# Moving the starts of TensorE's moving operands inside their SBUF tiles in a fused attention and mixture-of-experts kernel

## The chip, the cores and the metric

One NeuronCore of one Trainium2 chip runs the whole kernel. The metric is the device time of one execution in microseconds. A run of the kernel before is shown by its median over three runs; a separate execution, taken with the hardware profiler, gives the trace.

## The reference

Two branches read the same x (2048 tokens, 512 features) and are mixed by a gate:

```
x = A_x;  g = sigmoid((x * gate_w).sum(-1))
a = attention(x):   qkv = x @ wqkv (512 x 1536), 32 heads of 16,
                    each position looks at 8 keys: itself and every second one before (window 8, dilation 2)
                    softmax, weighted sum of v, then @ wo
b = experts(x):     logits = x @ w_gate; the best 2 of 8 experts per token
                    out += gate * (silu(x @ w1[e]) @ w2[e])      w1: 512 x 1376, w2: 1376 x 512
return g * a + (1 - g) * b
```

## The kernel before, in words

All products keep float32 accuracy with operands split in two (a high and a low part in fp32r): a product is hi*hi + hi*lo + lo*hi, so three matmuls stand where one would.

*Stage 1, qkv.* The columns of wqkv come in four chunks c of 384. For each chunk 16 token blocks j pass through `qkv_mm`: 12 matmuls each (4 k slices, 3 combinations), the x block stationary (`xh`, `xl`), the weights `WH[c]`, `WL[c]` moving. Chunk 0 carries ten more columns (the expert logits and the gate), so its k slices lie 394 columns apart and its matmuls have 394 columns. The tiles of the weights have two places each for high and low, used in turn, in the pool `pa`.

*Routing and attention.* VectorE does routing, then attention by element-wise products, as filler: `att_fill` puts its pieces between other VectorE work by a cost model of TensorE's time (T_MM and others), so the order on VectorE is fixed when the program is built.

*Stage 2, experts.* Experts are ranked by load; rank R has room for CAPS[R] tokens: 558, 548, 534, 500, 500, 496, 484, 484. They run in the order ORD = 3, 0, 1, 2, 5, 6, 7, 4. An expert has 11 units f (128 of the 1376 hidden columns each). For a unit, `g1_mm` issues the first product (line 859): w1 stationary, the gathered rows of x (`xgh`, `xgl`, 4 k slices) moving, 12 matmuls of CAPS[R] columns, or 24 of half the width when that is over 512. `g1_act` (lines 869 to 873) makes h = silu in the tile `hs`, high part from column 0, low part from column 640; two hs tiles of 1152 columns serve in turn. `g2_mm` issues the second product. For R in TURN (0, 1, 2, 5, 6, 7) w2 is stationary and hs moves, MAIN[R] columns (496, 484, 472 for R = 0, 1, 2), lines 898, 899, 901; the first unit's first matmul of each of the four groups has 512. The tokens past MAIN[R] are done by two matmuls of 512 columns in which hs is stationary (lines 903, 904). For R = 3 and 4 hs is stationary and w2 moves, always 512 columns (lines 889 to 892). The rows lie in tiles of 4 x 576 columns; where CAPS[R] is at most 512 the k slices are 512 columns apart, from the tile's first column. In each unit the order on TensorE is: first product of the next unit, then second product of this one.

*Stage 3, output.* `wo_mm` multiplies the attention output with wo for 16 blocks j; the results of blocks 0 to 2 lie in the three PSUM banks "h", the rest in the five banks "y". `mix(j)` on VectorE joins block j with the sum over experts (read back from DRAM in five loads, `load_acc`) and sends it out. MIX says after which block's matmuls which blocks are mixed.

Tiles of one pool and tag share a place in SBUF, one after the other. In the pool `at`, "acc", "o" and "qt" hold attention tiles from the second chunk on; before that "acc" holds `ii` (an iota from which `ident` and `before` are made) and "o" the gate weights `wgs`.

Of the kernel before, what the change touches and what calls it, by code (L numbers as in the profile page):

```python
# [7 lines left out]
F32 = mybir.dt.float32  # L8
F32R = mybir.dt.float32r
# [9 lines left out]
P = 128  # L19
S = 2048  # L20
D = 512
NJ = S // P
KD = D // P
# [5 lines left out]
NF = 11  # L29

CAPS = [558, 548, 534, 500, 500, 496, 484, 484]
MAIN = [496, 484, 472] + CAPS[3:]

ORD = [3, 0, 1, 2, 5, 6, 7, 4]
# [2 lines left out]
NB = 5  # L37
N5 = sum(c > 4 * P for c in CAPS)
W_ = 4 * len(CAPS) + N5
NOV = 40  # L40
# [1 line left out]
FC = [min(P, F - P * f) for f in range(NF)]  # L42
CRPAD, PAPAD = 176, 32
NWARM, NWARM2 = 26, 4
MIX = {5: (0,), 6: (1, 2, 3), 7: (4,), 8: (5, 6), 9: (7, 8)} | {j: (j - 1,) for j in range(10, NJ - 1)} | {NJ - 1: (NJ - 2, NJ - 1)}
SPLIT = {1: (8, 10, 12, 14), 2: (4, 6, 8, 10)}
IDLE = 2.0
FILL = 0.5
# [16 lines left out]
def kernel(  # L65
# [37 lines left out]
    def py(name):  # L103
        return ps.tile([P, 512], F32, tag="y", bufs=5, name=name)

    def ph(name):
        return ps.tile([P, 512], F32, tag="h", bufs=3, name=name)
# [3 lines left out]
    at = phT.enter_context(tc.tile_pool(name="at", bufs=1, side="right"))  # L111
# [5 lines left out]
    pa = phA.enter_context(tc.tile_pool(name="pa", bufs=1, side="left"))  # L117
# [4 lines left out]
    for i in range(2):  # L122
        t = pa2.tile([P, 2, D], F32, tag="xr", bufs=2, name=f"xr{i}")
        XR[2 * i], XR[2 * i + 1] = t[:, 0], t[:, 1]

    NW = [394, 384, 384, 384]
# [9 lines left out]
                              wq[:, k, :, c * P:(c + 1) * P])  # L136


    wgs = at.tile([P, KD * 9], F32, name="wgs", tag="o")
    nc.scalar.dma_start(wgs[:, :KD * 8], w_gate.rearrange("(p k) e -> p (k e)", p=P))  # L140
    nc.scalar.dma_start(wgs[:, KD * 8:], gate_w.rearrange("(p k) -> p k", p=P))
    for j in range(2):
# [44 lines left out]
    for r in range(E):  # L187
        nc.gpsimd.memset(caps[:, r:r + 1], float(CAPS[r]))
    src = cp.tile([P, 2, NJ, 2], I32, name="src")
# [31 lines left out]
    def clear_acc(j):  # L221
        n = 4 if j == 12 else 2
        if j % 2 == 0 and j < 14:
            nc.sync.dma_start(acc_d[:S].rearrange("(p j) d -> p j d", p=P)[:, j:j + n], zer[:, None, :].to_broadcast([P, n, D]))

    def split_w(c, k, vec=False):
        if c not in WH:
            for W, n in ((WH, "wh"), (WL, "wl")):
                t = pa.tile([P, 1600], F32R, tag=n, bufs=2, name=f"{n}{c}")
                W[c] = t[:, :KD * NW[c]].rearrange("p (k c) -> p k c", k=KD)  # L230
        if k is None:
            return
        if vec:
            nc.vector.tensor_copy(WH[c][:, k, :384], WR[c][:, k, :384])
        else:
            nc.scalar.activation(WH[c][:, k, :384], WR[c][:, k, :384], AF.Copy)
        nc.vector.tensor_tensor(WL[c][:, k, :384], WR[c][:, k, :384], WH[c][:, k, :384].bitcast(F32), op=OP.subtract)
# [147 lines left out]
    def slots():  # L385
# [42 lines left out]
        V.tensor_scalar(io, cap, 4.0 * P, 4.0 * P, op0=OP.is_le, op1=OP.mult)  # L428
        for c, m in zip(CAPS[:N5], MAIN):
            V.tensor_scalar(rr, cap, float(c), float(m), op0=OP.is_equal, op1=OP.mult)  # L430
# [326 lines left out]
    def blocks(R):  # L757
        return [P] * 3 + [MAIN[R] - 3 * P] + [CAPS[R] - MAIN[R]] * (CAPS[R] > MAIN[R])

# [12 lines left out]
    HS, XGH, XGL = [], {}, {}  # L772
# [5 lines left out]
    def turn_rows(R, b):  # L778
        if b == 0:
            pool = B["01"[ORD.index(R) % 2]]  # L780
            w = 576 if CAPS[R] > 4 * P else 4 * P
            for X, tag in ((XGH, "xgh"), (XGL, "xgl")):
                X[R] = pool.tile([P, KD * 576], F32R, tag=tag, name=f"{tag}{R}")[:, :KD * w].rearrange("p (k c) -> p k c", k=KD)
        m = blocks(R)[b]
        n = -(-m // 32)
        o = min(b * P, MAIN[R])
        s = slice(o, o + m)
        raw = B["0"].tile([P, KD, P], F32, tag="xraw", bufs=2, name=f"xraw{R}_{b}")[:, :, :32 * n]
        V.transpose(raw.rearrange("p k (t i) -> p t k i", i=32), XG[R, b][:, :n].rearrange("p t (k q) -> p t k q", k=KD))
        clk["dve"] += T_S  # L790
        return XGH[R][:, :, s], XGL[R][:, :, s], raw[:, :, :m]
# [71 lines left out]
    def g1_act(R, f, i):  # L863
        tiles, halves = PH.pop((R, f))
        C = CAPS[R]
        hs = HS[i % 2]
        s = B["1"].tile([P, 576], F32, tag="hsf", bufs=2, name=f"hsf{R}_{f}")
        for t, (o, n) in zip(tiles, halves):
            nc.scalar.activation(hs[:, o:o + n], t[:, :n], AF.Silu)  # L869
        for t, (o, n) in zip(tiles, halves):  # L870
            nc.scalar.activation(s[:, o:o + n], t[:, :n], AF.Silu)  # L871
        n = MAIN[R]
        V.tensor_tensor(hs[:, 640:640 + n], s[:, :n], hs[:, :n].bitcast(F32), op=OP.subtract)  # L873
        if C > n:
            V.tensor_tensor(hs[:, n + 64:C + 64], s[:, n:C], hs[:, n:C].bitcast(F32), op=OP.subtract)
# [3 lines left out]
    def g2_mm(R, f, i):  # L879
        if f == 0:  # L880
            PY[R] = [py(f"py{R}_{b}") for b in range(4 + (CAPS[R] > MAIN[R]))]
        hs = HS[i % 2]
        wh, wl = WS.pop((2, R, f))
        y = PY[R]
        st, sp = f == 0, f == NF - 1
        if R not in TURN:

            for b in range(4):
                nc.tensor.matmul(y[b], hs[:, b * P:b * P + P], wh, start=st, stop=False)
                nc.tensor.matmul(y[b], hs[:, b * P:b * P + P], wl, start=False, stop=False)  # L890
            for b in range(4):
                nc.tensor.matmul(y[b], hs[:, 640 + b * P:640 + b * P + P], wh, start=False, stop=sp)
            return
        n = MAIN[R]
        for m in range(4):
            a, b = wh[:, m * P:m * P + P], wl[:, m * P:m * P + P]
            k = 4 * P if st else n
            nc.tensor.matmul(y[m][:, :k], a, hs[:, :k], start=st, stop=False)  # L898
            nc.tensor.matmul(y[m][:, :n], b, hs[:, :n], start=False, stop=False)  # L899
        for m in range(4):  # L900
            nc.tensor.matmul(y[m][:, :n], wh[:, m * P:m * P + P], hs[:, 640:640 + n], start=False, stop=sp)  # L901
        if CAPS[R] > n:
            nc.tensor.matmul(y[4], hs[:, n:n + P], wh, start=st, stop=False)
            nc.tensor.matmul(y[4], hs[:, n:n + P], wl, start=False, stop=sp)
# [95 lines left out]
    for c in range(1, 4):  # L1000
        for j in range(NJ):
# [41 lines left out]
            if c == 3:  # L1043
                los()
                for g, u in NEXTW.pop(j - 1, ()):
                    g(*u)
                if j == 10:
                    prep_w1(*units[0])
                    NEXTW[j] = ((next_w1, units[0]),)
                if 7 <= j < 7 + len(blocks(ORD[0])):  # L1050
                    split_rows(*turn_rows(ORD[0], j - 7))
                if j == 13:

                    nc.scalar.activation(act0, ones[:, :1], AF.Silu)
                if 10 < j < 15:
                    u = units[(j - 10) // 2]
                    a, b = (prep_w1, next_w1) if j % 2 == 0 else (prep_w2, next_w2)
                    a(*u)
                    NEXTW[j] = ((b, u),)
# [5 lines left out]
    HS += [pb.tile([P, 1152], F32R, name=f"hs{i}") for i in range(2)]  # L1065
    n = 512 - CAPS[ORD[0]]
    for t in HS:
        for o, m in ((512, P), (1152, n)):
            V.tensor_tensor(t[:, o - n:o - n + m], ident[:, :m], ident[:, :m], op=OP.subtract)
    los()  # L1070
    WO = {}
# [30 lines left out]
    load_w2(ORD[0], 3)  # L1102
    NU = len(units)
    g1_act(*units[0], 0)
    for i, (R, f) in enumerate(units):
        C = CAPS[R]
# [6 lines left out]
        if R in NEXT:  # L1113
            N1 = NEXT[R]

            n = len(blocks(N1))
# [24 lines left out]
        if new_x:  # L1141
            rows = turn_rows(NEXT[R], f - 3)
# [7 lines left out]
        if i + 1 < NU:  # L1150
            g1_mm(*units[i + 1])
            g1_act(*units[i + 1], i + 1)
        if f == 3:
            read_back(f)
        if new_x:
            split_rows(*rows)
        g2_mm(R, f, i)
        out = y_out(R) if f == NF - 1 else iter(())
        next(out, None)
# [33 lines left out]
    def mix(j):  # L1193
        r = AG[j]
        n = D if j < NJ - 1 else D // 2
        for c in range(0, D, n):
            V.scalar_tensor_tensor(r[:, c:c + n], PA[j][c][:, :n], GG[:, j:j + 1], r[:, c:c + n],
                                   op0=OP.mult, op1=OP.add)
            nc.sync.dma_start(ot[:, j, c:c + n], r[:, c:c + n])
# [10 lines left out]
    for j in range(NJ):  # L1210
# [6 lines left out]

        for jj in MIX.get(j, ()):
            mix(jj)
# [7 lines left out]
    with tc.For_i(0, nov, 1) as it:  # L1227
# [25 lines left out]
        p = ph("pvx")  # L1253
# [5 lines left out]
        for f in range(NF):  # L1259
            m = FC[f]  # L1260
# [5 lines left out]
        for f in range(NF):  # L1266
            m = FC[f]
# [33 lines left out]
```

## Time and profile before

| | |
|---|---|
| median of three runs | 700.82 us (699.17 to 701.88) |
| the profiled execution's own time | 701.67 us |
| its span, first to last instruction | 699.9 us |
| TensorE matmuls (PE) busy | 685.4 us, 98% |
| VectorE (DVE) busy | 628.5 us, 90% |
| ScalarE (ACT) busy | 339.1 us, 48% |
| GpSimd (POOL) busy | 310.1 us, 44% |
| mean granted TensorE clock | 0.992 of 2.4 GHz |

Busy time is the union of an engine's instructions. The records of neighbouring matmuls overlap, so how long one matmul holds TensorE is read from the distance of their starts and not from the mean of one record.

### The profile page before, as it was taken

The page shows a single profiled execution, that of the slowest core. Times are in us where ns is not written, and L with a number is a line of the kernel's source. Part 1 is how long each engine was busy: PE and PEld are TensorE (multiplying, and loading weights), DVE is VectorE, ACT ScalarE, POOL GpSimd, SP SyncE. Part 2 cuts the span into 40 slices and gives each one's busy share as a digit, 9 for nine tenths or more (in the row PEclk, how much of TensorE's full clock was granted, in tenths as well). Part 3 has the DMA queues.
Part 4 walks back from the last instruction along what each step waited for, and adds up shares of the span by engine and source line. Part 5 has one row for each costly group of instructions (what it writes and reads, how often), then busy time and mean ns, then how long its engine had stood idle before and what let it go on. Part 6 is the DMA issues. An engine that isn't in the chain of part 4 may idle for free. (4 is left out here: it accounts for less than half of the span.)

```text
span 699.9 us, 11125 instructions
## 1 busy us (share of the span) xinstructions
PE 685.4 (98%) x3624; PEld 615.1 (88%) x3624; DVE 628.5 (90%) x782; ACT 339.1 (48%) x789; POOL 310.1 (44%) x351
## 2 busy tenths in 40 slices
PE   9999959989999999999999999999999999999997
PEld 9999959988889999999999998888888888888886
DVE  6859609999999999999999999998999999999793
ACT  5643204345644445455545454646644654465450
POOL 5400275056158506746663475475368230050400
PEclk9999979999999999999999999999999999999999
DMA  7868937638675837767867687978769884871493
GB/s 186 234 173 275 290 84 196 159 112 225 154 182 163 171 78 174 197 180 129 218 170 190 134 199 204 181 205 219 187 139 239 219 159 123 236 127 58 60 347 136
DMA packets 103565, 124.45 MB, mean 178 GB/s; under 512 B 10145, under 2 KB 73985, under 8 KB 103121
## 3 DMA queue, kind: packets, MB, share of 16 engines
q1 hardware_dynamic: 93072, 104.22, 55.2%
q0 software_dynamic: 10144, 19.48, 15.4%
q8 instruction: 29, 0.48, 0.3%
q14 instruction: 32, 0.25, 0.1%
q10 hardware_dynamic: 288, 0.02, 0.0%
HBM read 87.12 MB, written 36.57 MB: 177 GB/s over the span
## 5 line engine op out<-in xcount | busy, mean ns | idle before, releaser
L766 POOL DMA_INDIRECT xg<-in_A_x_dram,TQ x133 | 183.6, 1381 | 112.5 <-DVE rt_tk L519 51.1
L869 ACT ACTIVATE hs<-phh 128x500 fp32r<-128x500 f32 (+5 forms) x121 | 54.9, 481 | 156.8 <-PE phh L859 144.8
L898 PE MATMUL py<-hs,w2h 128*128 128x484 f32 (+3 forms) x264 | 100.7, 382 | 0.0
L899 PE MATMUL py<-hs,w2l 128*128 128x484 f32 (+2 forms) x264 | 100.6, 381 | 0.0
L859 PE MATMUL phh<-xgl,w1h 128*128 128x500 f32 (+5 forms) x484 | 96.3, 332 | 1.6 <-DVE xgl L804 1.6
L859 PE MATMUL phh<-xgh,w1h 128*128 128x500 f32 (+5 forms) x484 | 96.3, 332 | 0.5 <-ACT xgh L794 0.5
L859 PE MATMUL phh<-xgh,w1l 128*128 128x500 f32 (+5 forms) x484 | 96.2, 331 | 0.0
L911 POOL DMA_INDIRECT acc_d<-yr,TI x24 | 50.1, 2086 | 93.8 <-ACT yr L935 89.2
L859 PEld LDWEIGHTS phh<-xgh,w1h 128*128 128x128 f32 x484 | 78.6, 188 | 10.8 <-ACT xgh L794 0.8
L317 PE MATMUL pq<-wh,xh 128*128 128x384 f32 (+1 forms) x248 | 84.7, 342 | 1.9 <-issue 1.9
L317 PE MATMUL pq<-wl,xh 128*128 128x384 f32 (+1 forms) x248 | 83.9, 340 | 2.3 <-issue 2.3
L837 ACT ACTIVATE w2h<-w2r 128x512 fp32r<-128x512 f32 (+1 forms) x88 | 55.5, 631 | 60.6 <-PE py L901 20.5
L859 PEld LDWEIGHTS phh<-xgl,w1h 128*128 128x128 f32 x484 | 76.7, 188 | 9.2 <-DVE xgl L804 2.0
L859 PEld LDWEIGHTS phh<-xgh,w1l 128*128 128x128 f32 x484 | 76.8, 188 | 7.3
L317 PE MATMUL pq<-wh,xl 128*128 128x384 f32 (+1 forms) x248 | 77.6, 340 | 3.2 <-issue 3.2
L327 ACT ACTIVATE stg<-pq 128x128 f32<-128x128 f32 x192 | 40.1, 282 | 69.4 <-PE pq L317 47.7
L628 DVE TENSOR_TENSOR pr<-qt,kt 128x2048 f32<-128x2048 f32 x32 | 73.1, 2293 | 0.1
L631 DVE TENSOR_REDUCE lg<-pr 128x128 f32<-128x2048 f32 x32 | 72.4, 2271 | 0.0
L901 PE MATMUL py<-hs,w2h 128*128 128x484 f32 (+2 forms) x264 | 68.5, 381 | 0.0
L873 DVE TENSOR_TENSOR hs<-hsf,hs 128x484 fp32r<-128x484 f32 (+3 forms) x88 | 58.9, 670 | 5.2 <-ACT hsf L871 5.1
L804 DVE TENSOR_TENSOR w2l<-w2r,w2h 128x512 fp32r<-128x512 f32 (+1 forms) x88 | 60.5, 687 | 0.0
L804 DVE TENSOR_TENSOR w1l<-w1r,w1h 128x512 fp32r<-128x512 f32 (+1 forms) x88 | 59.3, 674 | 0.1
(235 smaller groups left out, 1282.3 us busy)
## 6 DMA issues: line engine op xcount, KB each, us to landing
w2r<-in_B_w_dram SPq DMA_DIRECT2D x40, 512.0 KB
w1r<-in_B_w_dram SPq DMA_DIRECT2D x96, 192.0 KB
qkv<-stg SPq DMA_DIRECT2D x24, 512.0 KB
ysc<-yt SPq DMA_DIRECT2D x24, 256.0 KB
yr<-ysc SPq DMA_DIRECT2D x6, 1024.0 KB
kt<-qkv SPq DMA_DIRECT2D x32, 156.0 KB
vt<-qkv SPq DMA_DIRECT2D x32, 156.0 KB
qt<-qkv SPq DMA_DIRECT2D x32, 128.0 KB
```

The costliest lines, as they stand in the source:

```text
L317: nc.tensor.matmul(p[:, :n], xx[j][:, s], ww[c][:, k, :n], start=(q == 0), stop=(q == 3 * KD - 1))
L628: V.tensor_tensor(pr, qb, custom(k, 4 * u * DH, [[2 * DH, 2], [1, 1024]]), op=OP.mult)
L631: V.tensor_reduce(lg[:, :, 2 * u - 2:2 * u].rearrange("p a w -> p w a"), prs[u - 1].rearrange("p w (a d) -> p w a d", d=16), axis=AX.X, op ...
L766: nc.gpsimd.indirect_dma_start(out=t[:, T], out_offset=None, in_=xq, in_offset=bass.IndirectOffsetOnAxis(ap=TQ[:, T, col:col + 1], axis=0))
L804: V.tensor_tensor(l, t, h.bitcast(F32), op=OP.subtract)
L837: nc.scalar.activation(hh, tt, AF.Copy)
L859: nc.tensor.matmul(t[:, :n], w[:, k], xx[:, k, o:o + n], start=(k == 0 and i == 0), stop=(k == KD - 1 and i == 2))
L869: nc.scalar.activation(hs[:, o:o + n], t[:, :n], AF.Silu)
L873: V.tensor_tensor(hs[:, 640:640 + n], s[:, :n], hs[:, :n].bitcast(F32), op=OP.subtract)
L898: nc.tensor.matmul(y[m][:, :k], a, hs[:, :k], start=st, stop=False)
L899: nc.tensor.matmul(y[m][:, :n], b, hs[:, :n], start=False, stop=False)
L901: nc.tensor.matmul(y[m][:, :n], wh[:, m * P:m * P + P], hs[:, 640:640 + n], start=False, stop=sp)
```

## The change

Four things move; no product, no column count and no order of the experts changes.

1. Where the moving operands of the experts begin. `SHIFT`: the rows of expert 3 begin 48 columns into their tiles, those of 4 at 32, of 6 and 7 at 48. `HSHIFT`: h of experts 0, 1, 2, 6 and 7 begins 8 columns into the hs tile (the low part at 648). One more strip of each hs tile, 12 columns, is zeroed at the start (columns 628 to 640).
2. The weights of chunk 0 get tiles of their own, in the places "acc" and "o" of `at`, from column 112, with the k slices 448 columns apart instead of 394. Chunks 1 and 3 share one place in `pa`, chunk 2 has the other.
3. `wgs` is put into the place "qt" instead of "o".
4. `MIX`: block 3 is mixed first and block 4 next, then 0 and 1, then 2; before it was 0, then 1, 2 and 3, then 4.

```
+SHIFT = {3: 48, 4: 32, 6: 48, 7: 48}
+HSHIFT = {0: 8, 1: 8, 2: 8, 6: 8, 7: 8}
...
-MIX = {5: (0,), 6: (1, 2, 3), 7: (4,), 8: (5, 6), 9: (7, 8)} | {j: (j - 1,) for j in range(10, NJ - 1)} | {NJ - 1: (NJ - 2, NJ - 1)}
+MIX = {5: (3,), 6: (4, 0, 1), 7: (2,), 8: (5, 6), 9: (7, 8)} | {j: (j - 1,) for j in range(10, NJ - 1)} | {NJ - 1: (NJ - 2, NJ - 1)}
...
-    wgs = at.tile([P, KD * 9], F32, name="wgs", tag="o")
+    wgs = at.tile([P, KD * 9], F32, name="wgs", tag="qt")
...
+    def w_tile(n, c):
+        t = pa.tile([P, 1600], F32R, tag=f"{n}{c % 2}", name=f"{n}{c}")
+        return t[:, :KD * 384].rearrange("p (k c) -> p k c", k=KD)
+
     def split_w(c, k, vec=False):
         if c not in WH:
             for W, n in ((WH, "wh"), (WL, "wl")):
-                t = pa.tile([P, 1600], F32R, tag=n, bufs=2, name=f"{n}{c}")
-                W[c] = t[:, :KD * NW[c]].rearrange("p (k c) -> p k c", k=KD)
+                if c == 0:
+                    for i in (2, 1):
+                        W[i] = w_tile(n, i)
+                    t = at.tile([P, 2048], F32R, tag={"wh": "acc", "wl": "o"}[n], name=f"{n}0")
+                    W[c] = t[:, 112:112 + KD * 448].rearrange("p (k c) -> p k c", k=KD)
+                elif c == 3:
+                    W[c] = w_tile(n, c)
...
-                X[R] = pool.tile([P, KD * 576], F32R, tag=tag, name=f"{tag}{R}")[:, :KD * w].rearrange("p (k c) -> p k c", k=KD)
+                X[R] = pool.tile([P, KD * 576], F32R, tag=tag, name=f"{tag}{R}")[:, SHIFT.get(R, 0):][:, :KD * w].rearrange("p (k c) -> p k c", k=KD)
...
-        hs = HS[i % 2]
+        hs = HS[i % 2][:, HSHIFT.get(R, 0):]
...
-        for o, m in ((512, P), (1152, n)):
+        for o, m in ((512, P), (640, n), (1152, n)):
```

The line of hs changes alike in `g1_act` and `g2_mm`.

## Rows read from the trace of the kernel before

**Rows 1.** The page's first part, busy us of each engine (share of the span) and instructions.

```profile
PE 685.4 (98%) x3624; PEld 615.1 (88%) x3624; DVE 628.5 (90%) x782; ACT 339.1 (48%) x789; POOL 310.1 (44%) x351
```

**Rows 2.** Busy time by stretch. Columns: stretch, its length, busy us (instructions) of PE, PEld, DVE, ACT and POOL, granted clock, busy share of the DMA engines, GB/s. The second stretch holds the eight experts.

```profile
93.00:108.00 15.00, 7.58 (x26) 6.35 (x25) 2.69 (x2) 3.78 (x17) 12.09 (x23) 0.66 0.20 55
156.50:660.00 503.50, 503.50 (x2618) 442.55 (x2619) 491.04 (x559) 266.33 (x531) 252.29 (x219) 1.00 0.72 170
```

**Rows 3.** Starts of matmuls on TensorE, from the timeline at ten places. Columns: start in us, length of the merged records in us, engine, line, operation, out<-in, stationary and moving shape, how many are merged. Between two rows of a pair lie only matmuls of the first row's shape: 12 for chunk 0 (394 columns), 12 for chunk 2 (384), 12 and 2 for expert 0, 24 for expert 1, 12 for expert 2, 24 for expert 5, 24 for expert 6, 12 and 12 for expert 4.

```profile
14.92 0.34 PE L317 MATMUL pq<-wh,xh 128*128 128x394 f32 x1
...
17.10 0.34 PE L317 MATMUL pq<-wh,xh 128*128 128x394 f32 x1
...
85.92 0.33 PE L317 MATMUL pq<-wh,xh 128*128 128x384 f32 x1
...
88.00 0.33 PE L317 MATMUL pq<-wh,xh 128*128 128x384 f32 x1
...
235.84 0.39 PE L898 MATMUL py<-hs,w2h 128*128 128x496 f32 x1
...
238.53 0.40 PE L903 MATMUL py<-w2h,hs 128*128 128x512 f32 x1
...
239.00 0.94 PE L859 MATMUL phh<-xgh,w1h 128*128 128x280 f32 x6
...
301.08 1.17 PE L859 MATMUL phh<-xgh,w1h 128*128 128x274 f32 x8
...
304.12 0.38 PE L898 MATMUL py<-hs,w2h 128*128 128x484 f32 x1
...
370.99 0.37 PE L898 MATMUL py<-hs,w2h 128*128 128x472 f32 x1
...
373.55 0.39 PE L903 MATMUL py<-w2h,hs 128*128 128x512 f32 x1
...
432.06 1.04 PE L859 MATMUL phh<-xgh,w1h 128*128 128x496 f32 x4
...
437.34 0.60 PE L859 MATMUL phh<-xgh,w1h 128*128 128x496 f32 x2
...
484.91 1.04 PE L859 MATMUL phh<-xgh,w1h 128*128 128x484 f32 x4
...
490.16 0.38 PE L859 MATMUL phh<-xgh,w1h 128*128 128x484 f32 x1
...
600.69 1.06 PE L859 MATMUL phh<-xgh,w1h 128*128 128x500 f32 x4
...
603.37 0.39 PE L889 MATMUL py<-w2h,hs 128*128 128x512 f32 x1
...
606.09 0.38 PE L859 MATMUL phh<-xgh,w1h 128*128 128x500 f32 x1
```

**Rows 4.** Groups of instructions by line and form. Columns: line, engine, operation, out<-in, shapes, count | busy us, mean ns of one | idle us before them.

```profile
L899 PE MATMUL py<-hs,w2l 128*128 128x484 f32 x132 | 50.3, 381 | 0.0
...
L859 PE MATMUL phh<-xgh,w1h 128*128 128x500 f32 x88 | 23.4, 387 | 0.5 <-ACT xgh L794 0.5
...
L1069 DVE TENSOR_TENSOR hs<-ident 128x12 fp32r<-128x12 f32 x2 | 0.3, 157 | 0.0
```

**Rows 5.** The start of the kernel on VectorE (the second reader of ii) and on ScalarE (the first write of the first chunk's weight tile). In brackets: idle us before it, and what ended the wait.

```profile
1.28 0.72 DVE L179 TENSOR_SCALAR before<-ii 128x128 bf16<-128x128 int32 x1
...
3.82 0.23 ACT L244 ACTIVATE wh<-wgs 128x32 fp32r<-128x32 f32 x1 [0.64 <-DMA wgs<-in_B_w_gate_dram]
```

**Rows 6.** VectorE at the first expert: the strips of hs are zeroed, then the first low part of h is made.

```profile
160.91 0.64 DVE L1069 TENSOR_TENSOR hs<-ident 128x128 fp32r<-128x128 f32 x4
162.18 0.68 DVE L873 TENSOR_TENSOR hs<-hsf,hs 128x500 fp32r<-128x500 f32 x1 [0.62 <-ACT hsf L871]
```

**Rows 7.** The output stage: the mixes of blocks 1, 2 and 3 on VectorE, then TensorE as block 8 begins (line 1189 at 673.84).

```profile
671.66 2.04 DVE L1197 SCALAR_TENSOR_TENSOR ag<-pa,GG,ag 128x512 f32<-128x512 f32 x3
...
673.54 0.39 PE L1191 MATMUL pa<-woh,w1l_o 128*128 128x512 f32 x1
673.84 0.47 PE L1189 MATMUL pa<-woh,w1h_o 128*128 128x512 f32 x1
674.15 0.40 PE L1190 MATMUL pa<-wol,w1h_o 128*128 128x512 f32 x1
```

**Rows 8.** VectorE's waits from 110 to 660 us (who waited <- for whom: us in total, times, longest), and the timeline of expert 7: VectorE's low part of h (line 873), and the matmuls that read it (line 901).

```profile
DVE hs L873 <- ACT hsf L871: 5.1, 7, 1.3
DVE mx L652 <- ACT lg L642: 4.1, 4, 1.6
...
553.77 0.69 DVE L652 TENSOR_REDUCE mx<-lg 128x64 f32<-128x512 f32 x1 [0.82 <-ACT lg L642]
...
562.01 0.66 DVE L873 TENSOR_TENSOR hs<-hsf,hs 128x484 fp32r<-128x484 f32 x1
...
562.81 1.07 PE L901 MATMUL py<-hs,w2h 128*128 128x484 f32 x4
...
567.18 0.66 DVE L873 TENSOR_TENSOR hs<-hsf,hs 128x484 fp32r<-128x484 f32 x1
...
568.09 1.04 PE L901 MATMUL py<-hs,w2h 128*128 128x484 f32 x4
```

**Rows 9.** TensorE between 93 and 104.5 us, one of its matmuls and the wait before it.

```profile
98.54 0.48 PE L317 MATMUL pq<-wh,xl 128*128 128x384 f32 x1 [2.31 <-issue]
```

More of the change, by code (lines that the diff above doesn't have):

```diff
@@ L881, in g2_mm @@
             PY[R] = [py(f"py{R}_{b}") for b in range(4 + (CAPS[R] > MAIN[R]))]
-        hs = HS[i % 2]
+        hs = HS[i % 2][:, HSHIFT.get(R, 0):]
         wh, wl = WS.pop((2, R, f))
```

## The prediction

> **What bounds the kernel now.** I read the page first. TensorE's matmuls are busy for 685.4 of 699.9 us and VectorE for 628.5 [rows 1]; the reader is to see that TensorE hardly pauses, so that other engines matter only where it waits for them, and that VectorE comes next. The table by stretches says where: from 156.5 to 660 us, the eight experts, PE is busy in 503.50 of 503.50 us and VectorE in 491.04 [rows 2]. No wait is left there to be removed. So the end is set by how many matmuls there are and how far apart they start. The program issues the same 3624 matmuls after the change; only the distance of their starts can move.
>
> That distance is not the 381 or 387 ns that the grouped rows give as the mean of one (those overlap); it is read from the timeline, as time between two starts divided by the matmuls between them [rows 3]. The granted clock is 1.00 there [rows 2], which is 2.4 GHz, so n columns need n/2.4 ns; what is above that I call the surplus:
> - 512 columns, last expert: 606.09 - 603.37 = 2.72 us for 12, 226.7 ns, surplus 13.3. 496, expert 5: 437.34 - 432.06 = 5.28 us for 24, 220.0, surplus 13.3. 384: 88.00 - 85.92 for 12, 173.3, surplus 13.3.
> - 484, expert 6: 490.16 - 484.91 for 24, 218.75, surplus 17.1. 500, expert 4: 603.37 - 600.69 for 12, 223.3, surplus 15.0. 472, expert 2: 373.55 - 370.99 for 12, 213.3, surplus 16.7. 496, but expert 0: 238.53 - 235.84 for 12, 224.2, surplus 17.5. 394: 17.10 - 14.92 for 12, 181.7, surplus 17.5.
> - the halves of a 548-slot expert: 304.12 - 301.08 for 24, 126.7, surplus 12.5. And the two 512-column matmuls behind expert 0, whose weights lie in the hs tile: 239.00 - 238.53 for 2, 235, surplus 21.7.
>
> So 484 columns cost nearly as much as 496, and 496 cost 220.0 in one expert and 224.2 in another: the column count alone does not give the surplus. The second group of widths is just the one the change moves.
>
> At this point a rule of the Trainium skill speaks against the change. "TensorE: Matmul & The Clock Gate", section "Back-to-back issue gap", gives the distance from the columns alone (N/2.4 + 2.5 ns), and Part 2, "What happens when you issue a matmul", has the weight load on a port of its own that takes nothing from the moving stream. By it a tile's place could not matter and the matmuls would gain nothing. The rows do not agree: it would put 496 columns at 209.2 ns in both experts, where they stand at 220.0 and 224.2.
>
> **The change, part by part.** The matmuls moved, from the loops (11 units of an expert, 12 matmuls of a product; the groups by form agree: 132 for one of three second-product parts, 88 for one of three parts of the first product [rows 4]): with 484 columns 2 x 11 x 12 = 264 in the first product and, in the second, 3 x 132 less the 12 that read 512, 384; with 500, 264; with 496 in expert 0 and with 472 in expert 2, 132 less 4 each, 128; with 394, 16 blocks x 12 = 192.
> - *The unknown price* is the surplus at the new places, which no row shows. Bounds: below, the next lower multiple of 6.67 ns, because every steady distance in [rows 3] whose tiles all start alike is one (173.3, 220.0, 226.7 are 26, 33 and 34 of them; 223.3 is the mean of 33 and 34): 484 at 213.3, 500 at 220.0, 472 at 206.7, 394 at 173.3. Above, the worst surplus seen, 21.7. In between lies the surplus that the cleanest full-width groups have, 13.3, and I take it, since the moved matmuls have the same operands as those groups and are nearest to them in width.
> - 484: 218.75 to 215.0, 648 x 3.75 ns = 2.43 us. 500: 223.3 to 221.7, 264 x 1.7 = 0.44. Expert 0's 496: 224.2 to 220.0, 128 x 4.2 = 0.53. 472: 213.3 to 210.0, 128 x 3.3 = 0.43. The 22 matmuls behind expert 0: 235 to 226.7, 0.18.
> - 394: the wider tile (stride 448 for 394) lets all four k slices start alike, as the 384 ones do; I take the whole step above 13.3, 27 x 6.67 = 180.0, so 192 x 1.7 = 0.32 us.
> - *Where that tile now lies.* It takes the places of "acc" and "o". It must wait for the readers of ii, the last of which ends at 1.28 + 0.72 = 2.00 us; its first write comes at 3.82, held by the load of the gate weights [rows 5]. Cost nothing; without that cover this write would be later by what the wait exceeds 3.82. The loads and issues of wgs are the same two. In the second stretch cols0 and cols1 take the places after the first chunk's last matmul, long before.
> - *The zeroed strip.* Two more VectorE instructions of 128x12 at 157 ns, 0.31 us [rows 4], in front of the first hs. VectorE stands idle 0.62 us just behind them [rows 6], which hides them; uncovered they would put 0.3 us before the second product.
> - *Blocks 3 and 4 first.* At 673.54 and 673.84 two matmuls take 0.30 and 0.31 us to the next instead of 0.227: block 8 waits for the bank that block 3's mix frees, third in a run of mixes that ends at 671.66 + 2.04 = 673.70 [rows 7]. With block 3 mixed first that wait goes: 0.15 us. The same 17 mixes and 17 output DMAs are issued in the same queue; blocks 0 to 2 hold banks that nothing needs. The first mix still waits for the same load of acc, so nothing is late in its place; if block 8 still waited, the edit would be worth nothing.
> - *VectorE as the next bound.* TensorE's gain counts only if VectorE keeps up. From 110 to 660 us its two largest waits add up to 9.2 us, both for ScalarE work that follows a matmul [rows 8]; those shrink when the matmuls come sooner. The tight place is expert 7: hs is ready at 562.01 + 0.66 = 562.67 for a matmul at 562.81, and at 567.84 for one at 568.09, leads of 0.14 and 0.25 us, after a VectorE wait of 0.82 us that ends at 553.77 [rows 8]. Between these points TensorE would gain (562.81 - 553.77) / 5.25 units x 24 x 3.75 ns = 0.15 us: at the edge. I take 0.1 us off.
>
> Sum: 2.43 + 0.44 + 0.53 + 0.43 + 0.18 + 0.32 + 0.15 - 0.1 = 4.4 us. The profiled execution took 701.67 us (span 699.9 and 1.8 around it), 0.85 above the median 700.82 of the runs shown; 701.67 - 4.4 = 697.3 for a run like it, and **696.4 us** against the median.
>
> **Rivals.**
> 1. *The whole lower step* (the lower bounds): 648 x 5.45 = 3.53, 264 x 3.3 = 0.88, 128 x 4.2 = 0.53, 128 x 6.7 = 0.85, 192 x 8.4 = 1.61, with 0.18 and 0.15 it is 7.7 us; expert 7 would then lose some 0.3 to VectorE: 693.4 us. For it: the halves have a surplus of 12.5, under 13.3, so 13.3 is no floor. Against it: 484 at 213.3 would have 11.7, which no row shows.
> 2. *Places do not set the surplus*, or one group gains what another loses: 0.3 us from the tail and little more, 699.5 to 700.8. For it: the same 496 columns at the same kind of place differ in experts 5 and 0, so what ran before may matter more than the place; 384 columns are at 173.3 although other chunks' tiles lie elsewhere. By the rule of the Trainium skill quoted above the outcome would be this one.
> 3. *The new places are worse* (the other side). The 235 ns row shows that another offset between the two operands can cost 21.7. If all moved matmuls went there: 648 x 4.6 + 264 x 6.7 + 128 x 4.2 + 128 x 5 + 192 x 4.2 ns = 6.7 us, 707.5; if about half did, 704. It decides (over 0.5%) from a mean of 3.5 us / 1360 = 2.6 ns per moved matmul. Against it: nine of the ten readings lie below that surplus.
> 4. *The stall moves.* From 93 to 104.5 us TensorE's matmuls come with waits of up to 2.31 us between them, with "issue" as the reason, and from 93 to 108 PE is busy 7.58 of 15 us at a granted clock of 0.66, partly on the lower level of 1.2 GHz [rows 2, 9]. I see no cause that the change touches and leave it. Were its 11.5 us gone, 684.9; were they doubled, 707.9.
>
> **How the numbers follow.** About 0.5% (3.5 us) is what a measurement of this kernel can tell from no change. Forecast 0.40, first rival 0.15, second 0.28, third 0.13, fourth 0.04, half of it each way. The forecast's own spread (gains of 3 to 5.5 us) crosses 3.5, so I count a tenth of it to "same" and a tenth of the second rival to "faster": faster 0.56, same 0.29, slower 0.15. The range has to reach into the first rival and through the second: 692.8 leaves out about 0.07 below, 702.8 about 0.11 above. The likeliest case alone is 695 to 698.
>
> **What would show it.** In expert 6 two first products one unit apart, 24 matmuls, should start 5.16 us apart or less instead of 5.25; in expert 4 the 12 of 500 columns 2.66 instead of 2.68, or 2.64; in expert 0 the 12 of 496 columns 2.64 instead of 2.69; in expert 2 the 12 of 472 2.52 instead of 2.56; the 12 of 394 2.16 instead of 2.18. Expert 5's first product should stay at 220.0. At block 8 the gap of 0.15 us is gone. PE's waits for hs in expert 7 stay under 0.3 us. The forecast is wrong if 484 columns stay at 218 or rise, if VectorE's lag shows as new waits of PE, or if the stall at 93 us has another length.

## The result

The changed kernel took 705.46 us (median of nine, 703.22 to 707.25) beside 701.97 for the kernel before on the same chip (nine, 699.17 to 703.70): a ratio of 1.0053, 95% interval 1.0035 to 1.0070. Forecast was 696.4. Four later comparisons, two of the changed kernel on chips without a stall at 93 us, one on a chip with it, and one with the stall imitated, gave ratios of 1.0014, 1.0014, 1.0010 and 1.0013. So the change itself costs about 1 us (0.87 to 1.05 between the medians of the four), where I expected a gain of 4.4; 2.5 us more lie in the first comparison alone. The ratios are not those of the medians: they leave out two far slower executions, of 754.78 and 1755.40 us, both in the last comparison.

First the engines' busy time on the page of the changed kernel, and the busy time of the stall and of the experts (columns as in [rows 2]):

```profile
PE 688.4 (98%) x3624; PEld 615.2 (87%) x3624; DVE 628.8 (89%) x784; ACT 339.3 (48%) x789; POOL 310.5 (44%) x351
```

```profile
93.00:108.00 15.00, 7.81 (x26) 6.56 (x25) 2.40 (x2) 3.75 (x17) 11.95 (x23) 0.61 0.19 53
155.00:664.00 509.00, 506.60 (x2621) 442.69 (x2621) 494.01 (x565) 268.69 (x538) 254.94 (x220) 1.00 0.71 168
```

The count of matmuls is the same [rows 1]; the stall is there as in [rows 2], the granted clock in it 0.61 instead of 0.66. Starts of matmuls from the timeline of the changed kernel answer to [rows 3]. From one row to the next of a group are 12 matmuls, 2 between the last two rows of expert 0, and 24 where the first product of expert 5 comes twice (line 328 was 317, 870 was 859, 909 was 898, 900 was 889, 914 was 903):

```profile
14.86 0.34 PE L328 MATMUL pq<-wh,xh 128*128 128x394 f32 x1
...
17.02 0.34 PE L328 MATMUL pq<-wh,xh 128*128 128x394 f32 x1
...
236.17 0.40 PE L909 MATMUL py<-hs,w2h 128*128 128x496 f32 x1
...
238.88 0.39 PE L914 MATMUL py<-w2h,hs 128*128 128x512 f32 x1
...
239.34 0.41 PE L870 MATMUL phh<-xgh,w1h 128*128 128x280 f32 x2
...
371.64 0.38 PE L909 MATMUL py<-hs,w2h 128*128 128x472 f32 x1
...
374.20 0.40 PE L914 MATMUL py<-w2h,hs 128*128 128x512 f32 x1
...
433.00 0.60 PE L870 MATMUL phh<-xgh,w1h 128*128 128x496 f32 x2
...
438.27 1.04 PE L870 MATMUL phh<-xgh,w1h 128*128 128x496 f32 x4
...
492.55 1.04 PE L870 MATMUL phh<-xgh,w1h 128*128 128x484 f32 x4
495.19 0.39 PE L909 MATMUL py<-hs,w2h 128*128 128x484 f32 x1
...
497.80 0.60 PE L870 MATMUL phh<-xgh,w1h 128*128 128x484 f32 x2
...
603.50 1.07 PE L870 MATMUL phh<-xgh,w1h 128*128 128x500 f32 x4
606.22 0.39 PE L900 MATMUL py<-w2h,hs 128*128 128x512 f32 x1
...
608.99 0.62 PE L870 MATMUL phh<-xgh,w1h 128*128 128x500 f32 x2
```

Expert 6, first product of 484: 2.64 us for 12, 220.0 ns, where 218.75 stood and 215.0 was forecast; its second product 2.61, 217.5. Expert 4: 500 columns 2.72, 226.7, where 223.3 stood and 221.7 was forecast; and the 512 columns behind them, which nothing moved, 2.77, 230.8, where 226.7 stood. Expert 0: 496 columns 2.71, 225.8 instead of 224.2. Expert 2: 472 columns 2.56, as before. Expert 5 keeps 5.27 for 24. Only two kinds came out as forecast: 394 columns, 2.16, 180.0, and nearly the two matmuls behind expert 0, 0.46 for 2, 230 instead of 235.

TensorE's waits from 85 to 660 us in the changed kernel (for whom: us in total, times, longest), and the stretch in which VectorE comes late to expert 6:

```profile
PE pq L328 <- issue: 7.2, 5, 2.2
PE phh L870 <- DVE xgl L815: 1.5, 1, 1.5
PE py L912 <- DVE hs L884: 0.9, 1, 0.9
```

```profile
481.82 0.72 DVE L977 STREAM_TRANSPOSE yt<-py 128x512 f32<-128x512 f32 x1 [1.85 <-DMA xg<-in_A_x_dram,TQ]
483.21 2.16 DVE L977 STREAM_TRANSPOSE yt<-py 128x512 f32<-128x512 f32 x3 [0.68 <-remote]
...
490.86 0.66 DVE L884 TENSOR_TENSOR hs<-hsf,hs 128x484 fp32r<-128x484 f32 x1
...
491.57 0.70 PE L912 MATMUL py<-hs,w2h 128*128 128x484 f32 x2 [0.90 <-DVE hs L884]
```

VectorE's transposes of expert 5's result wait 1.85 us, put down to a gather of rows, and 0.68 us, put down to no engine of this core ("remote"). Some 8 to 10 us later TensorE pays 0.90 us for an hs that is late, and with the first unit of expert 6 it is 1.7 us in all. In the profile before, these transposes wait for nothing and TensorE has no wait there.

Adding up the distances from start to start, stage by stage, the two profiles differ by 3.4 us: chunk 2 with its stall +0.8, the wait at expert 6 +1.7, expert 4 +0.9, expert 0 +0.2, expert 2 +0.2, expert 1 +0.1, experts 6 and 7 without the wait +0.15, expert 5 +0.07, expert 3 -0.2 (its waits included), chunk 0 +0.3 (its 394 columns are faster, but two starts lie 0.6 us apart at 32 us), chunk 3 -0.65 (a single wait of 0.65 us that the changed kernel does not have), and the output stage -0.17. The places explain less than half of that; the experiments had to separate the two.

### The profile page after: what moved, and what is told of

It reads as the page before. It is cut to its first block, busy times and chain, and to the rows that moved or that the text cites. A ratio compares the mean times of both kernels' runs of the same rounds, so it can differ in the third digit from the quotient of the medians.

```text
span 703.3 us, 11127 instructions
## 1 busy us (share of the span) xinstructions
PE 688.4 (98%) x3624; PEld 615.2 (87%) x3624; DVE 628.8 (89%) x784; ACT 339.3 (48%) x789; POOL 310.5 (44%) x351
## 5 line engine op out<-in xcount | busy, mean ns | idle before, releaser
L777 POOL DMA_INDIRECT xg<-in_A_x_dram,TQ x133 | 187.6, 1410 | 112.7 <-DVE rt_tk L530 51.4
```

Of the source, the lines that this page charges most:

```text
L777: nc.gpsimd.indirect_dma_start(out=t[:, T], out_offset=None, in_=xq, in_offset=bass.IndirectOffsetOnAxis(ap=TQ[:, T, col:col + 1], axis=0))
```

## Experiments

**Theory A**: the new places are worse than the ones before, because the place sets the surplus otherwise than I assumed. **Theory B**: the stalls belong to the change, whatever the places do. The first three runs undo parts of the change.

The first leaves rows and h where they were; the first chunk's tile and the order of the mixes stay changed:

```diff
-SHIFT = {3: 48, 4: 32, 6: 48, 7: 48}
-HSHIFT = {0: 8, 1: 8, 2: 8, 6: 8, 7: 8}
+SHIFT = {}
+HSHIFT = {}
```

> The changed kernel with the rows and h left where they were before: of the change only the wider tile of the first chunk's weights (and the gate weights' other place) and the order of the mixes are left. Theory A (the moved places cost the time: summed over their stages in the two profiles the moved rows cost 1.0 us, the moved h 0.3): this kernel is within 0.5 us of the kernel before, 484 columns stand at 218.7 ns again in the first product of experts 6 and 7, 500 at 223.5 in expert 4, and the second product of expert 4 at 226.8. Theory B (not the places but stalls that the rest of the change brings or shifts: 1.7 us at 484 to 492 us, where VectorE comes late to the second product of expert 6, and 0.8 us more in the stall at 93 us): it stays 2 us or more above the kernel before, with the stall of expert 6 still there.

The second keeps `SHIFT` and empties `HSHIFT`:

> The changed kernel with h left at its old place; the rows of experts 3, 4, 6 and 7 moved. Theory A: 1.0 us above the first kernel of this call (first products: expert 3 -0.6, experts 6 and 7 +0.2 each, expert 4 +0.4; second products, whose operands did not move, behind expert 3 +0.4 and expert 4 +0.4), with 220.0 ns for 484 columns and 226.8 for 500 in expert 4. Theory B: the same as the first kernel within 0.3 us.

The third keeps `HSHIFT` and empties `SHIFT`:

> The changed kernel with the rows left at their old place; h of experts 0, 1, 2, 6 and 7 moved by 8 columns. Theory A: 0.3 us above the first kernel of this call (second product of expert 0 at 226.4 ns, of expert 2 at 216.8, of experts 6 and 7 at 218.3), and the second products of experts 3 and 4 at 226.8 again. Theory B: the same as the first kernel within 0.3 us, unless the stall of expert 6 comes with the moved h; then 1.5 us or more above it.

The chip was another: the kernel before took 688.80 us there, with no stall at 93 us. Nothing moved: 688.25 (ratio 0.9994, 0.9985 to 1.0003). Rows alone: 689.08, +0.83. h alone: 688.84, +0.59. Theory B has no place here: without the moves the rest of the change costs nothing and seems to save half a us (the interval still takes in no change). The changed kernel again, on the same kind of chip (its edit is a blank):

> The changed kernel itself once more. The first three runs came from a chip on which the kernel before takes 688.8 us instead of 702.0 and has no stall at 93 us. Theory A (only the moved places cost time; the first chunk's tile and the mixes save 0.5 us as in the first of them): the differences of the three runs add up, rows +0.8, h +0.6, and 0.2 where both meet, so 1.1 us above the kernel before on this chip, ratio 1.0016, with no stall at expert 6's second product. Theory B (the stalls belong to the change): ratio 1.004 to 1.005 as in the first comparison, with 1.7 us of waits at expert 6 in the trace.

689.78 beside 688.91, ratio 1.0014 (1.0005 to 1.0023), and no wait at expert 6. A sum over the stages shows where. The table has us from the first start of a product to the next product's, summed over an expert's 11 units, first / second product, for these four kernels and for two that come further down (the shifts of rows exchanged, and the places chosen by tables):

| expert (columns) | none moved | rows | h | both | shifts exchanged | by the tables |
|---|---|---|---|---|---|---|
| 3 (500) | 29.83 / 29.95 | 29.48 / 30.33 | 29.82 / 29.96 | 29.45 / 30.33 | 29.46 / 30.33 | 29.80 / 29.95 |
| 0 (halves, 496) | 34.07 / 34.52 | 34.07 / 34.52 | 33.93 / 34.87 | 33.93 / 34.87 | 34.07 / 34.52 | 34.07 / 34.52 |
| 1 (halves, 484) | 33.43 / 33.86 | 33.43 / 33.86 | 33.60 / 33.80 | 33.59 / 33.80 | 33.43 / 33.86 | 33.46 / 33.65 |
| 2 (halves, 472) | 32.57 / 33.20 | 32.57 / 33.21 | 32.61 / 33.39 | 32.61 / 33.39 | 32.57 / 33.20 | 32.58 / 33.31 |
| 5 (496) | 29.04 / 29.11 | 29.04 / 29.07 | 29.13 / 29.13 | 29.13 / 29.09 | 29.04 / 29.11 | 29.12 / 29.14 |
| 6 (484) | 28.87 / 28.93 | 29.01 / 28.91 | 28.88 / 28.90 | 29.04 / 28.82 | 28.55 / 28.91 | 28.47 / 28.51 |
| 7 (484) | 28.87 / 28.92 | 28.72 / 28.87 | 28.88 / 28.91 | 29.04 / 28.85 | 28.56 / 28.99 | 28.45 / 28.82 |
| 4 (500) | 29.49 / 29.94 | 29.94 / 30.36 | 29.56 / 29.93 | 29.94 / 30.36 | 29.17 / 30.33 | 29.57 / 29.96 |
| sum against none | 0 | +0.79 | +0.70 | +1.64 | -0.50 | -1.22 |
| measured | 0 | +0.83 | +0.59 | +1.5 | -0.5 | -1.2 |

The sums and the measured differences agree within 0.15 us. Expert 3 shows the pattern that I had missed: its 500 columns gain 0.35 us by the move, and the 512 columns of the second product behind them, unmoved, lose 0.38.

Then the disputed price by itself. A kernel of matmuls only: 24 in a row for each of five widths and nine places of the moving rows, behind a short matmul, the whole list twice:

> Not the kernel's computation: only matmuls of fp32r operands, 24 in a row of each kind with weights that change from one to the next, for 484, 500, 496, 472 and 512 columns with the moving rows at nine places (88, 8, 120, 96, 24, 0, 16, 104 and 80 floats past a multiple of 128) and the weights at four, the whole list run twice behind a matmul of 96 and of 104 columns. Theory A: the place of the moving rows sets the distance of starts: 484 columns 218.7 ns at place 88 and 220.0 at 8, 500 columns 223.3 at 88, 221 at 8 and 226.7 at 120, 512 columns 226.7 at 88; the two passes agree. Rival (what ran before sets it, not the place): the same column count has one distance at all places, or the two passes differ by 3 ns and more at the same place.

Rows of its timeline, a pair for each kind; from the start of the first row of a pair to that of the second are 13 distances (484 columns at places 88, 8 and 120, then 500 at 8 and 120, then 512 at 88 and 8, the weights always at 88):

```profile
16.80 3.00 PE L64 MATMUL py<-M,W 128*128 128x484 f32 x13
19.64 0.21 PE L59 MATMUL sp<-M,W 128*128 128x96 f32 x1
...
22.18 3.02 PE L64 MATMUL py<-M,W 128*128 128x484 f32 x13
25.04 0.20 PE L59 MATMUL sp<-M,W 128*128 128x96 f32 x1
...
27.52 2.96 PE L64 MATMUL py<-M,W 128*128 128x484 f32 x13
30.32 0.21 PE L59 MATMUL sp<-M,W 128*128 128x96 f32 x1
...
70.51 3.02 PE L64 MATMUL py<-M,W 128*128 128x500 f32 x13
73.37 0.21 PE L59 MATMUL sp<-M,W 128*128 128x96 f32 x1
...
75.98 3.11 PE L64 MATMUL py<-M,W 128*128 128x500 f32 x13
78.92 0.21 PE L59 MATMUL sp<-M,W 128*128 128x96 f32 x1
...
211.33 3.11 PE L64 MATMUL py<-M,W 128*128 128x512 f32 x13
214.28 0.21 PE L59 MATMUL sp<-M,W 128*128 128x96 f32 x1
...
216.95 3.19 PE L64 MATMUL py<-M,W 128*128 128x512 f32 x13
219.98 0.21 PE L59 MATMUL sp<-M,W 128*128 128x96 f32 x1
```

484 columns: 2.84 / 13 = 218.5 ns, 220.0, and 215.4; 500: 220.0 and 226.2; 512: 226.9 and 233.1. The matmuls, their number and their widths are the same in each pair; only the place differs. Distances of the second 12 of each kind in ns, by the offset of the moving rows from the weights' place modulo 64 floats (two values where the passes, or two places of one offset, differ; the first 12, right behind the short matmul, run 4 to 8 ns higher):

| columns | 0 | 8 | 16 | 32 | 40 | 48 | 56 |
|---|---|---|---|---|---|---|---|
| 484 | 218.3 to 218.8 | 216.7 | 220.5 | 215.6 | 220.0 | 220.0 | 218.8 |
| 500 | 223.2, 226.6 | 226.7 | 228.9 | 226.7 | 223.4 | 220.0 | 226.7 to 228.3 |
| 496 | 223.3 | 224.4 | 226.7 | 223.3, 226.7 | 223.4 | 220.0, 226.7 | 226.4 |
| 472 | 213.3 | 213.3 | 210.0 | 213.3 | 213.4 | 213.3 | 213.3 |
| 512 | 226.7 | 233.3 | 228.8 | 233.0 | 234.2 | 233.2 | 233.3 |

So Theory A holds for 484, 472 and 512 columns. For 500 and 496 the rival is right in part: at some offsets the same place gives distances 3 or 7 ns apart in the two passes.

It is the offset between the two operands and not the moving place alone: weights moved back by 16 instead of rows moved on by 16 give 220.5 for 484 columns as well (210.0 for 472, 229.4 for 512), and moving both to 8 gives 218.7 and 226.6, the values of offset 0. The change had put 484 columns at offset 48 (220.0 in the table, 220.0 in its trace) and 500 of expert 4 at 32 (226.7 and 226.7), and h at 8, good for 484 but not for 496. In this table the two shifts of rows look exchanged:

```diff
-SHIFT = {3: 48, 4: 32, 6: 48, 7: 48}
-HSHIFT = {0: 8, 1: 8, 2: 8, 6: 8, 7: 8}
+SHIFT = {3: 48, 4: 48, 6: 32, 7: 32}
+HSHIFT = {}
```

> The changed kernel with the two shifts of rows exchanged, 48 floats for the 500 columns of experts 3 and 4 and 32 for the 484 of experts 6 and 7, and h unmoved. By the table of the places run (second units): 484 columns 32 floats past the weights' place stand at 215.6 ns, and 500 columns 48 floats past it at 220.0. Theory A: first products of experts 6 and 7 at 215.6 to 216.5 (0.3 to 0.4 us less each than in the kernel with none moved), of experts 3 and 4 at 220 to 221 (0.35 and 0.45 less); the second products behind them pay a part back, 0.38 us each in experts 3 and 4; in all 0.4 to 0.9 us below the kernel with none moved. Rival (what one product gains, the one behind it loses, since every change of place costs some 35 ns): within 0.2 us of that kernel.

687.74 us beside 688.91 (ratio 0.9984, 0.9975 to 0.9993), 0.5 below the kernel with none moved. The first products do as the table says (484 at 216.3, 500 at 221.0); experts 3 and 4 pay it back in the second. What an alternation costs was measured at the same time, in units of 12 and 12 as an expert has them:

> Not the kernel's computation: units of 12 and 12 matmuls as an expert has them, the first product's moving rows and the second's each at a place of its own (0 to 48 floats past the weights' place, modulo 64), three units of each pair. Theory A: the sum of a unit is that of the two steady distances of the places run (484 columns: 218.3 at 0, 215.6 at 32, 216.7 at 8) plus 30 to 40 ns for each change of place within a unit: the lowest for 484 columns is 32 for both products, at 215.6 to 216. Rival: distances in units of two kinds do not follow from the steady ones; then the pairs of places rank otherwise.

For 484 columns, offset of the first and of the second product, mean distance over a unit in ns: 0 and 0 218.7, 32 and 0 217.5, 8 and 8 216.7, 32 and 32 215.6. For 500 and then 512: 0 and 0 225.0, 48 and 0 225.6, with 221.1 and 230.1 for the two parts, which is what experts 3 and 4 show in the kernel. For these, with one offset in both products nothing is paid between them; with 48 and 0 the 512 columns lose 3.5 ns each. Expectation and rival are both right in part: most steady values carry over, but the price of an alternation differs from pair to pair (32 and 8 for 484 columns wavers between 216.8 and 218.3). 496 columns carry over least: with both products at 40 they stand at 226.7, where the table has 223.4, and with both at 48 at 226.7 in all three units.

From the two tables follows a choice, for which the h tiles grow by 64 floats, taken from a pad:

```diff
-SHIFT = {3: 48, 4: 32, 6: 48, 7: 48}
-HSHIFT = {0: 8, 1: 8, 2: 8, 6: 8, 7: 8}
+SHIFT = {6: 32, 7: 32}
+HSHIFT = {1: 32, 2: 16, 6: 32, 7: 32}
...
-    lp.tile([P, 184], F32, name="lpad")
+    lp.tile([P, 56], F32, name="lpad")
...
-    HS += [pb.tile([P, 1152], F32R, name=f"hs{i}") for i in range(2)]
+    HS += [pb.tile([P, 1216], F32R, name=f"hs{i}") for i in range(2)]
```

> The wider first chunk and the order of the mixes kept; rows of experts 3 and 4 where they were; the rows and the h of experts 6 and 7 both 32 floats past the weights' place, h of expert 1 32 past it and of expert 2 16 past it (the h tiles 64 floats wider, taken from a pad on the left). From the two tables: 484 columns with both products at 32 stand at 215.6 ns and pay nothing between them, where the kernel with none moved has 218.7 and 219.1; 472 at 16 stand at 210.0. Theory A: 0.8 us less in each of experts 6 and 7, 0.2 in expert 1 and 0.3 in expert 2: 2.0 us below the kernel with none moved, so 2.6 us below the kernel before on a chip without the stall, ratio 0.996. Rival (the tables were taken without other engines at work and do not carry over): less than 1 us below it, with 484 columns above 217 ns.

687.01 us beside 688.81, ratio 0.9972 (0.9961 to 0.9982): faster than both kernels. Expert 6 in its timeline, 12 matmuls between neighbours:

```profile
481.96 1.02 PE L870 MATMUL phh<-xgh,w1h 128*128 128x484 f32 x4
484.55 0.38 PE L909 MATMUL py<-hs,w2h 128*128 128x484 f32 x1
487.13 0.38 PE L870 MATMUL phh<-xgh,w1h 128*128 128x484 f32 x1
```

5.17 us for 24, 215.4 ns, in both products. The stages chosen by the tables gave 1.4 us where 2.1 were expected: expert 7 lost 0.27 in three distances of its second product, where VectorE is now late with hs (the weight loads wait 0.5 us for it there), and expert 2 did not gain: its 472 columns came to 212.7 ns, not 210.0, and its 26 matmuls of 512 columns, which read h as weights in part, rose from 228.2 to 234.3. Matmuls behind halves are in no table. The last try of a place, `HSHIFT` with `0: 48` added:

> As the kernel above, and h of expert 0 (496 columns) 48 floats past the weights' place. The tables show 496 columns there in two states, 220.0 and 226.7 ns, in one pass the one and in the other the other; now expert 0's second product has 224.2 as mean of its 154. Theory A can only bound it: 0.3 us below the kernel above if the lower state holds, 0.6 us above it if the upper does; a mean between them would say that it changes from unit to unit.

687.36, 0.35 above; expert 0's 496 columns at 226.5 ns, none of the 128 distances under 225: the upper state throughout, as in the pairs. The changed kernel beside these two:

> The changed kernel as it is, beside the two above. Theory A: ratio 1.001 to 1.002 to the kernel before on a chip on which the kernel before takes 689 us; on a chip on which it takes 702 us and stalls at 93 us, 1.005 as in the first comparison, with waits of VectorE or a longer stall for the rest. Rival: 1.005 on either.

689.83, ratio 1.0014 (1.0005 to 1.0023), on another chip, which does not have the stall either.

Left is the excess of the first comparison. A stall can be imitated where it matters, for what comes behind it: 72 matmuls more at its place, which keep TensorE busy 12.5 us; the edit is the same in both kernels:

```diff
             qkv_mm(c, j, LOW2ND if (c, j) == (2, 0) else STEPS)
+            if (c, j) == (2, 7):
+                for _ in range(6):
+                    for q in range(3 * KD):
+                        k, i = STEPS[q]
+                        xx, ww = ((XH, WH), (XH, WL), (XL, WH))[i]
+                        nc.tensor.matmul(PQ[c, j][:, :384], xx[j][:, k * P:(k + 1) * P], ww[c][:, k, :384],
+                                         start=(q == 0), stop=(q == 3 * KD - 1))
```

> The kernel before with the 12 matmuls of block 7 of chunk 2 repeated six times (the last time counts), 72 matmuls of 384 columns, 12.5 us, at the place where the first comparison's chip stalls TensorE for 11 us; all that follows comes later by that, as there. 12.5 us above the kernel before if it is on a chip without the stall, 701.3; it is there for the next kernel to be compared with.

> The changed kernel with the same 72 matmuls. Theory A (of the first comparison's 3.5 us the places explain about 1, the rest is that chip's stall as it fell in those executions): 0.9 to 1.0 us above the kernel just before, as without the delay, and no wait at expert 6's second product. Rival C (the changed program, once it is late by 11 to 13 us against the DMA work, brings VectorE's transposes of expert 5 onto GpSimd's gathers for the expert after next, and TensorE pays): 2.5 us or more above it, with that wait in the trace.

701.44 and 702.38: 0.94 us between them, and TensorE has no wait at expert 6. Being late by itself does not bring the wait. At last the kernels came onto a chip with the real stall:

> The changed kernel as it is, once more. Theory A: 0.9 to 1.0 us above the kernel before (ratio 1.0014) on a chip where the kernel before takes 689 us; on one where it takes 702 us and stalls at 93 us, also about 1 us above it in the parts outside stalls, the stalls themselves scattered by some us from execution to execution. Rival: on a chip with the stall 1.005 again, with the stall of the changed kernel longer in every execution.

> Rows and h unmoved, the wider first chunk and the order of the mixes kept. Theory A: 0.5 us below the kernel before on either kind of chip, 1.5 below the kernel above. Rival: on a chip with the stall 2 us or more above the kernel before, which would put the longer stall down to the first chunk's part of the change.

The kernel before 700.15, the changed one 701.20 (ratio 1.0010, 0.9997 to 1.0024), the one with none moved 699.62 (0.9994, 0.9978 to 1.0010). The changed kernel's stall here, by stretch and by TensorE's waits:

```profile
93.00:108.00 15.00, 8.99 (x30) 7.24 (x30) 7.15 (x5) 3.06 (x14) 12.52 (x16) 0.66 0.28 76
```

```profile
PE pq L328 <- issue: 6.0, 6, 1.6
```

The stall is shorter than in [rows 2] (7.58 us busy there, 8.99 here), the granted clock the same 0.66, and no wait at expert 6 follows. So neither the longer stall nor that wait comes with the change every time. Of the nine executions of the changed kernel in the first comparison, five show a mean granted clock of 0.989 or 0.990 and took 705.1 to 707.3 us, the other four 0.992 or 0.993 and 703.2 to 705.9 us; eleven of the twelve here have 0.992 or 0.993. A part of the excess thus goes with a lower clock, as in the profile with its longer stall. Why it came in the first comparison, whose interval this one does not reach, is not settled, nor what the stall is: "issue" is all that the rows name.

## Why the prediction was wrong

The measured 705.46 us is 9.1 above the forecast of 696.4. Of that, 5.4 are the change's own 1 us in place of the 4.4 to be gained; this is the step below, and it is shown. 1.15 are the kernel before, which took 701.97 beside the changed one and not the 700.82 that the forecast started from. 2.5 are the excess of the first comparison, and their cause stays open.

- *What bounds the kernel*: right. On the chips without the stall TensorE has hardly a pause to lose, and every difference is one of distances: the sums over the stages give the measured differences within 0.15 us.
- *The unknown price*, the step that failed. I saw that the place matters, and then gave the new places the 13.3 ns of the cleanest groups, as nearest in width, without asking what is the same in those groups. The rows could not bear that: in the kernel before the moving rows and the weights of 484, 496, 500 and 512 columns all begin 88 floats past a multiple of 128, by the addresses of its program, and [rows 3] show 13.3 to 17.5 for them; one place never meant one surplus. What the runs put there is a table of width and offset. At the places of the change the surplus, as a mean over an expert's units, is 18.3 for 484 columns of rows (I took 13.3; 17.1 before), 18.5 for expert 4's 500, 12.6 for expert 3's 500 without its pauses, and for h 15.3 to 16.5 (484), 19.4 (496) and 17.2 (472).
- *One unit taken for all.* Expert 0's 496 columns were read at 224.2 ns in one unit [rows 3]. The next unit has 12 of them in 2.64 us, 220.0 ns:

```profile
242.09 0.38 PE L898 MATMUL py<-hs,w2h 128*128 128x496 f32 x1
...
244.73 0.40 PE L903 MATMUL py<-w2h,hs 128*128 128x512 f32 x1
```

  Over the 11 units of the kernel before they go 219.8, 223.6 and 224.2 in turn, 222.4 on average, at one and the same offset. So even 220.0 at the new place would have gained 0.3 us there and not 0.53, and place and width are not all that counts. What the period of three comes from no run shows.
- So the terms of the sum, from the table by stages: 484, forecast 2.43 less: first products 0.34 more, second ones 0.24 less. 500, forecast 0.44 less: 0.38 less in expert 3, 0.45 more in expert 4. Expert 0's second product, 0.71 less: 0.35 more (226.1 ns for 496; the matmuls behind it did fall, from 232.6 to 228.3). 472, 0.43 less: 0.19 more, about half of it in the 512 columns beside them (228.2 to 231.3). The moves together cost 1.5 us; what is left of the change (394 columns and mixes, forecast 0.47 less) gave 0.55 less.
- *What runs before counts.* I let each edit act on the matmuls that it moves. The 512 columns of experts 3 and 4 lost 0.38 and 0.42 us unmoved, expert 5's first product 0.09, because what runs before them changed. My second rival said this ("one group gains what another loses") and was bounded at +0 us; the third said the other side at 704 to 707.5. The change's own 1 us lies between them.
- *394 columns* and *blocks 3 and 4 first*: right. 180.0 ns, and at block 8 the gap is gone, as the output stage of the changed kernel shows against [rows 7]:

```profile
677.13 0.39 PE L1202 MATMUL pa<-woh,w1l_o 128*128 128x512 f32 x1
677.36 0.39 PE L1200 MATMUL pa<-woh,w1h_o 128*128 128x512 f32 x1
677.59 0.39 PE L1201 MATMUL pa<-wol,w1h_o 128*128 128x512 f32 x1
677.82 0.39 PE L1202 MATMUL pa<-woh,w1l_o 128*128 128x512 f32 x1
```

  Block 8 begins at 677.36. The four starts are 0.23 apart, where 0.30 and 0.31 stood.
- *VectorE as the next bound*: named rightly, but not reached by the change itself, which did not speed TensorE up. The kernel by the tables did, and paid 0.27 us in expert 7, where I had said.
- *The stall*, the fourth rival, was given 0.04. In the first comparison's profile it was 0.8 us longer, at a mean granted clock of 0.61 instead of 0.66, and the waits of 1.7 us at expert 6 came with it, which the prediction had only as a sign of being wrong. Neither came again in the later comparison.

The rule of the Trainium skill that spoke against the change ("TensorE: Matmul & The Clock Gate", "Back-to-back issue gap"), which the section gives for an isolated matmul, would make 204.2 ns of 484 columns at any place. The matmul kernel shows 215.6 to 220.5 there, by the place alone: that the change would gain nothing came true, but not for the rule's reason.

## What to carry to other kernels

A steady distance between matmuls is a property of the width, of the offset between moving rows and weights, and of what ran before: measure it at the new place, over all units and not in one, in a kernel of matmuls alone, before a place is chosen, choose both products of a loop together, and look again in the kernel itself, since not every value carries over (472 columns at offset 16 stood at 210.0 ns in the table and at 212.7 in expert 2). When an edit touches one group, add up the neighbours too. And repeat a comparison of half a per cent on another chip before a reason is sought for it: here 2.5 of 3.5 us did not come again.

## What the runs showed of the hardware

- For each of the five widths one of the measured offsets gives the least surplus, and it is the width modulo 64, rounded down to 16: 512 at 0 (13.3 ns), 496 at 48 (13.3, in one of its two states), 500 at 48 (11.7), 484 at 32 (13.9), 472 at 16 (13.3). That is a pattern of five widths at seven offsets, no mechanism.
- The same width and offset can hold several distances: 500 columns at offset 0 at 223.2 in one pass and 226.6 in the other; 496 at 220.0 in expert 5, 223.3 in the matmul kernel, and 219.8, 223.6 and 224.2 in turn in expert 0. Many values are whole multiples of 6.67 ns (213.3, 220.0, 226.7, 233.3) or means of neighbours.
- Chips differed by more than such a change: the kernel before took 688.8 to 688.9 us on three chips and 700 to 702 where TensorE's instructions stall at 93 us. Whether that belongs to the chip or to the time it was used no run separates.
